# Attention scores as three 64-row products in two halves of TensorE's array, pairs taken two at a time, z turned by VectorE

## The chip, the cores and the metric

One core of a Trainium2 chip runs the whole kernel. The metric is the device time of one execution in microseconds (us), the median of three runs. Engines are called TensorE (PE in the rows; PEld is its weight loads), VectorE (DVE), ScalarE (ACT), GpSimd (POOL) and SyncE (SP, which issues the DMAs; SPq is its queue).

## What is computed

An attention without softmax over two batches of 3008 tokens, then two networks of two layers on its result. All arrays are float32 (the weights arrive as float64 and are converted by the kernel).

```
def _attn_ref(u, v, z):                      # u, v: (2, 3008, 256), z: (2, 3008, 64)
    scores = (1.0 / S) * np.matmul(z, z.transpose(0, 2, 1))
    attn = np.maximum(scores, 0.0) ** 2
    out = np.matmul(attn, v)
    return u * out
def _moe_ref(x, w_in, w_out):                # 256 -> 2048 -> 256
    h = x @ w_in
    return (h - np.tanh(h)) @ w_out
# second network: g = h from 1 up, 0 from -1 down, (h + 1)^2 / 4 between; g @ w_out
```

## The kernel before

Every float32 operand is split into hi (12 significant bits) and lo (the rest), and a product is the sum of float32r products of such parts: ScalarE copies hi, VectorE subtracts to get lo (`split`, line 87).

The attention is a list of 144 pairs (b, c, t): batch b, chunk c of 512 queries (the last chunk has 448), and two tiles of 128 keys. For each pair `attn_s` (line 283) makes the scores of two key tiles against the query chunk in one two-bank PSUM tile `sc`: z is held with its 64 hi rows over its 64 lo rows (`zs`) and the other way round (`zw`), so that two 128-row products (lines 293, 294) take all four terms; four products a pair. ScalarE then makes r = relu(sc / S) (line 300) and hi = r squared (302), VectorE a = r times r (301) and lo = a - hi (303). Two pairs later (LAG) `attn_av` (line 307) makes 12 products with v (line 316) into `acc`. After 12 pairs of a chunk VectorE multiplies acc by the turned u (342).

The order of the work is the order of the program on each engine. The loop of line 557 does for each pair i: `pump(i)` (line 516), which starts and advances loads; the hooks (loads of u, line 247, and its turning, 266); `attn_s` of pair i; `attn_av` of pair i - 2; and some steps of the weights' conversion on VectorE. `flush` at the end of `attn_s` issues the lo halves of splits of loads, which `split` had put off.

Loads of z, v and later the weights go through four buffers of the pool `raw` (line 58), taken in turn, and end in one of 18 slots of `ring`. The DMA of a load is issued on SP's queue, in order, and waits there until the buffer's former content was split. z comes in groups of 1024 tokens: one DMA, a split, eight 128x128 transposes on TensorE (line 143) into a PSUM tile of the scores' pool, a copy to `zs`, and two DMAs that make `zw` (154, 155). Tokens are ordered with partition p holding tokens 23p to 23p + 22, so that a DMA reads long pieces; the 64 tokens left over of each batch are a tile of their own.

The two networks follow, 96 pairs each, with 24 products a pair on TensorE.

Of the kernel before, what the change touches and what calls it, by code (L numbers as in the profile page):

```python
# [8 lines left out]
F32 = mybir.dt.float32  # L9
F32R = mybir.dt.float32r  # L10
# [16 lines left out]
def attention_then_two_ffn(  # L27
# [21 lines left out]
    assert D == 2 * P and DQ == 64 and REST == 64 and NFULL % 2 == 1 and B == 2  # L49
    NT = B * S // P  # L50
# [9 lines left out]
    tmp_p = ctx.enter_context(tc.tile_pool(name="tmp", bufs=2))  # L60
    sp_p = ctx.enter_context(tc.tile_pool(name="split", bufs=3))
# [3 lines left out]
    ident0 = const.tile([P, P], F32, name="ident0")  # L65
    ident = const.tile([P, P], F32R, name="ident")
# [9 lines left out]
    loads = []  # L76
    deferred = []   # VectorE's halves of splits: a pair later than ScalarE's
# [23 lines left out]
    def load_z(b, g):  # L101
        """Group g of 8 token tiles of z: [zh; zl] and [zl; zh], columns are tokens."""
        st = {}

        def dma(at=0, n=8):
            t = st["raw"] = raw_p.tile([P, 512], F32, tag="raw", name=f"zraw{b}_{g}_{at}")
            t3 = t.rearrange("p (t d) -> p t d", d=DQ)
            whole = min(n, NFULL - 8 * g - at)
            t0 = 8 * g + at
            nc.sync.dma_start(  # L110
                out=t3[:, :whole, :],
                in_=z[b, : NFULL * P, :].rearrange("(p t) d -> p t d", t=NFULL)[:, t0 : t0 + whole, :],
            )
            if whole < n:
                for h in range(2):
                    nc.sync.dma_start(out=t3[64 * h : 64 * h + 64, whole, :], in_=z[b, NFULL * P :, :])
            return t3

        def cut(at=0, n=8):
            t3 = st["raw"].rearrange("p (t d) -> p t d", d=DQ)  # L120
            zn = st["zn"] = sp_p.tile([P, 1024], F32R, tag="hi", name=f"zn{b}_{g}_{at}")
            if n < 8:
                zn = zn[:, : 3 * n * DQ].rearrange("p (t h d) -> p t h d", h=3, d=DQ)
            else:
                zn = zn.rearrange("p (t h d) -> p t h d", h=2, d=DQ)
            st["zn"] = zn
            split(zn[:, :, 0, :], zn[:, :, 1, :], t3[:, :n], now=(n < 8))
            if n < 8:
                nc.scalar.activation(out=zn[:, :, 2, :], in_=t3[:, :n], func=AF.Copy)

        def turn(at=0, n=8):
            flush()
            zn = st["zn"]
            ps = ps_s.tile([P, 2, 512], F32, tag="s", name=f"zps{b}_{g}_{at}")
            pw = ps_a.tile([P, 2, 512], F32, tag="acc", name=f"zpw{b}_{g}_{at}") if n < 8 else ps
            if at == 0:
                a = ring.tile([P, 1024], F32R, tag="w", name=f"zs{b}_{g}")
                w = ring.tile([P, 1024], F32R, tag="w", name=f"zw{b}_{g}")
                zs[b, g] = (a, w)
            a, w = zs[b, g]  # L140
            for i in range(8):
                h, k = divmod(i, n)
                nc.tensor.transpose(  # L143
                    (pw if h else ps)[:, i // 4, (i % 4) * P : (i % 4 + 1) * P].bitcast(F32R),
                    zn[:, k, h : h + 2, :].rearrange("p h d -> p (h d)"),
                    ident,
                )
            c = slice(at * P, (at + n) * P)
            got = ps.rearrange("p a n -> p (a n)")[:, : n * P]
            nc.scalar.activation(out=a[:, c], in_=got, func=AF.Copy)  # L150
            if n < 8:
                nc.vector.tensor_copy(out=w[:, c], in_=pw[:, 1, :])
            else:
                nc.sync.dma_start(out=w[0:64, c].bitcast(F32), in_=a[64:128, c].bitcast(F32))
                nc.sync.dma_start(out=w[64:128, c].bitcast(F32), in_=a[0:64, c].bitcast(F32))

        return [(dma, AHEAD), (cut, 3 if b + g == 1 else 4), (turn, 1 if b + g == 1 else 2)]

    def load_v(b, t):
        """Token tiles 2t and 2t+1 of v: hi and lo. The rest's tile holds hi over lo instead."""  # L160
        st = {}

        def dma():
            r = st["raw"] = raw_p.tile([P, 512], F32, tag="raw", name=f"vraw{b}_{t}")
            r3 = r.rearrange("p (t d) -> p t d", d=D)
            n = min(2, NFULL - 2 * t)
            nc.sync.dma_start(
                out=r3[:, :n, :],
                in_=v[b, : NFULL * P, :].rearrange("(p t) d -> p t d", t=NFULL)[:, 2 * t : 2 * t + n, :],
            )  # L170
# [71 lines left out]
    NPA = (NFULL + 1) // 2  # L242
    QC = (S + 511) // 512
# [3 lines left out]
    def load_u(b, c, j):  # L247
        """u transposed in blocks of 32: the load places the blocks, VectorE turns each."""
        n = min(4, NFULL - 4 * c)
        if j == 0:  # L250
            us[b, c] = (u_p.tile([P, 4, 4, 2, 32], F32, tag="ub", name=f"ub{b}_{c}"), n)
# [362 lines left out]
```

## Time and profile before

| what | value |
|---|---|
| median of 3 runs | 1570.79 us (1570.47 to 1572.19) |
| span of the profiled execution | 1569.2 us |
| PE busy | 1559.3 us (99%) |
| DVE busy | 1103.8 us (70%) |
| ACT busy | 777.4 us (50%) |
| chain that ended last | PE 99% |

The profiled execution's own time is not listed beside its span; the runs' median lies 1.6 us above the span, which is what lies around it. The scores' lines 293 and 294 are 8% of the chain that ended last, the products with v (316) 24%, the networks' products 67%. The attention ends, and the first network's products begin, at 519 us.

### The profile page before, as it was taken

The numbers are of one execution on the slowest core, as the hardware profiler recorded it, in microseconds if no ns is written. First come the engines' busy times: TensorE is split into PE (matmuls) and PEld (weight loads), VectorE is DVE, ScalarE is ACT, GpSimd is POOL, SyncE is SP. The second block draws the span as 40 slices with busy tenths as digits, with TensorE's granted clock in tenths as the row PEclk, the third lists the DMA queues.
The fourth block names the chain that finished last, engine by engine and source line by source line (L and its number), as shares of the span: only waits on it lengthen the run. The fifth ranks groups of instructions, "written<-read, shape, count | busy, mean of one in ns | idle before, by whom it ended". The sixth has DMA issues, their size and how long they took to land.

```text
span 1569.2 us, 19350 instructions
## 1 busy us (share of the span) xinstructions
PE 1559.3 (99%) x8057; PEld 1349.3 (86%) x8057; DVE 1103.8 (70%) x1132; ACT 777.4 (50%) x797; POOL 1.2 (0%) x7
## 2 busy tenths in 40 slices
PE   8999999999999999999999999999999999999998
PEld 6888889888888888888888888999999999999998
DVE  7888888888888966665665444477666666666665
ACT  7655557655556644444444444454444444444443
POOL 0000000000000000000000000000000000000000
PEclk9999999999999999999999999999999999999999
DMA  5121124221222311100101000020000000000000
GB/s 134 51 51 40 35 57 118 66 57 31 54 54 67 113 41 41 41 29 33 41 28 34 0 1 7 14 61 14 14 1 14 14 14 14 14 14 14 1 15 24
DMA packets 77400, 57.62 MB, mean 37 GB/s; under 512 B 54272, under 2 KB 55552, under 8 KB 77312
## 3 DMA queue, kind: packets, MB, share of 16 engines
q1 hardware_dynamic: 77312, 56.38, 12.6%
q8 instruction: 63, 1.03, 0.3%
q14 instruction: 25, 0.20, 0.0%
HBM read 39.19 MB, written 14.55 MB: 34 GB/s over the span
## 4 chain that ended last, share of the span: by engine, by line
PE 99%; DVE 0%; DMA 0%; ACT 0%; issue 0%; POOL 0%; SPq 0%; DVEq 0%; POOLq 0%
PE acc L316 24%; PE acc L416 17%; PE acc L396 16%; PE h L364 11%; PE h L365 11%; PE h L366 11%; PE sc L293 4%; PE sc L294 4%; PE zps L143 0%; PE warm L499 0%; DMA zw<-zs 0%; DVE lo L303 0%; DVE a L301 0%; ACT r L300 0%; PE zpw L143 0%
## 5 line engine op out<-in xcount | busy, mean ns | idle before, releaser
L88 ACT ACTIVATE gh<-g 128x1024 fp32r<-128x1024 f32 (+1 forms) x192 | 200.3, 1043 | 269.4 <-DVE g L383 141.3
L364 PE MATMUL h<-xl,w_in 128*128 128x512 f32 (+1 forms) x768 | 296.4, 386 | 0.0
L365 PE MATMUL h<-xh,w_in 128*128 128x512 f32 (+1 forms) x768 | 296.4, 386 | 0.0
L366 PE MATMUL h<-xh,w_in 128*128 128x512 f32 (+1 forms) x768 | 295.4, 385 | 0.0
L316 PE MATMUL acc<-hi,v 128*128 128x512 f32 (+1 forms) x1128 | 274.9, 385 | 0.0
L91 DVE TENSOR_TENSOR gl<-g,gh 128x1024 fp32r<-128x1024 f32 (+1 forms) x192 | 230.0, 1198 | 61.6 <-ACT gh L88 61.6
L316 PEld LDWEIGHTS acc<-hi,v 128*128 128x128 f32 x1128 | 211.7, 188 | 39.9 <-ACT hi L302 0.3
L378 DVE TENSOR_SCALAR t<-h 128x1024 f32<-128x1024 f32 (+1 forms) x96 | 115.4, 1202 | 170.9 <-PE h L366 170.9
L300 ACT ACTIVATE r<-sc 128x1024 f32<-128x1024 f32 (+1 forms) x144 | 145.4, 1010 | 175.0 <-PE sc L294 174.8
L375 DVE TENSOR_TENSOR g<-h,t 128x1024 f32<-128x1024 f32 (+1 forms) x96 | 115.4, 1202 | 146.2 <-ACT t L373 146.2
L301 DVE TENSOR_TENSOR a<-r 128x1024 f32<-128x1024 f32 (+1 forms) x144 | 172.5, 1198 | 49.8 <-ACT r L300 49.6
L416 PEld LDWEIGHTS acc<-w_out,gh 128*128 128x128 f32 x1504 | 192.8, 191 | 6.7
L416 PE MATMUL acc<-w_out,gh 128*128 128x256 f32 x1504 | 195.4, 283 | 0.0
L303 DVE TENSOR_TENSOR lo<-a,hi 128x1024 fp32r<-128x1024 f32 (+1 forms) x144 | 173.3, 1203 | 19.8 <-ACT hi L302 1.1
L396 PE MATMUL acc<-gh,w_out 128*128 128x512 f32 (+1 forms) x768 | 186.4, 385 | 0.0
L381 ACT ACTIVATE t<-t 128x1024 f32<-128x1024 f32 (+1 forms) x96 | 100.1, 1043 | 162.4 <-DVE t L378 162.4
L373 ACT ACTIVATE t<-h 128x1024 f32<-128x1024 f32 (+1 forms) x96 | 96.8, 1008 | 159.9 <-PE h L366 159.7
L366 PEld LDWEIGHTS h<-xh,w_in 128*128 128x128 f32 x768 | 144.3, 188 | 28.2
L396 PEld LDWEIGHTS acc<-gh,w_out 128*128 128x128 f32 x768 | 143.4, 188 | 27.5
L364 PEld LDWEIGHTS h<-xl,w_in 128*128 128x128 f32 x768 | 144.6, 188 | 25.3
L365 PEld LDWEIGHTS h<-xh,w_in 128*128 128x128 f32 x768 | 144.5, 188 | 24.2
L302 ACT ACTIVATE hi<-r 128x1024 fp32r<-128x1024 f32 (+1 forms) x144 | 150.4, 1045 | 9.2 <-PE acc L316 2.6
(61 smaller groups left out, 1421.1 us busy)
## 6 DMA issues: line engine op xcount, KB each, us to landing
wide_in<-in_moe_w_in_dram SPq DMA_DIRECT2D x16, 512.0 KB, 3.8
wide_out<-in_moe_w_out_dram SPq DMA_DIRECT2D x16, 512.0 KB, 3.8
vraw<-in_v_dram SPq DMA_DIRECT2D x22, 256.0 KB, 2.9
ub<-in_u_dram SPq DMA_DIRECT2D x160, 32.0 KB, 2.2
out_dram<-o SPq DMA_DIRECT2D x10, 512.0 KB, 2.6
w_in<-m_in SPq DMA_DIRECT2D x16, 256.0 KB, 2.2
w_out<-m_out SPq DMA_DIRECT2D x16, 256.0 KB, 2.1
wraw_in<-w_in SPq DMA_DIRECT2D x16, 256.0 KB, 2.9
```

What stands on the lines that cost most here:

```text
L88: nc.scalar.activation(out=hi, in_=src, func=AF.Copy)
L91: nc.vector.tensor_tensor(out=lo, in0=src, in1=hi.bitcast(F32), op=ALU.subtract)
L300: nc.scalar.activation(out=r[s], in_=ps[s], func=AF.Relu, scale=SCALE)
L301: nc.vector.tensor_tensor(out=a[s], in0=r[s], in1=r[s], op=ALU.mult)
L302: nc.scalar.activation(out=hi[s], in_=r[s], func=AF.Square)
L303: nc.vector.tensor_tensor(out=lo[s], in0=a[s], in1=hi.bitcast(F32)[s], op=ALU.subtract)
L316: nc.tensor.matmul(acc[:, d, :n], lhsT, g[:, j, :n], start=start, stop=stop)
L364: nc.tensor.matmul(ps[:, j, :n], w[:, 0, k, fs], xl[:, k, :n], start=(k == 0), stop=False)
L365: nc.tensor.matmul(ps[:, j, :n], w[:, 1, k, fs], xh[:, k, :n], start=False, stop=False)
L366: nc.tensor.matmul(ps[:, j, :n], w[:, 0, k, fs], xh[:, k, :n], start=False, stop=(k == 1))
L396: nc.tensor.matmul(acc[:, d, :n], w[:, part, j, d * P : (d + 1) * P], g[:, j, :n], start=start, stop=stop)
L416: nc.tensor.matmul(acc4[:, tt, :], g[:, j, tt * P : (tt + 1) * P], w[:, part, j, :], start=start, stop=stop, skip_group_check=True,)
```

## The change

z is loaded in groups of 512 tokens, in natural order, as 32x32 blocks by four DMAs: the two halves of its 64 columns, each to two places, so that the partitions 64 to 127 hold the same as 0 to 63. VectorE turns each block (`zt`), and hi and lo of it are two halves of one slot of the ring. The transposes on TensorE, the identity and the two DMAs for `zw` are gone. A group of z is loaded by one step (`work`) that issues its turning and both halves of its split at once.

The scores of a pair are six products of 64 rows: hi by hi, hi by lo, lo by hi, each for key tile 0 on partitions 0 to 63 and key tile 1 on partitions 64 to 127. `attn_s` takes two pairs: 12 products, two relus, two squares in place, two splits (hi is now a copy of a, after the square), and then two `attn_av`. The pools are: `tmp` one tag in 3 buffers (before two tags in 2), `split` 4 buffers (before 3), `raw` 4 as before. u, v and the output are in natural order: two DMAs of u for each step (before four or six), one store for each chunk. The networks write g in place of t. The start loads z, v 0 and v 1, with 7 products of zeros meanwhile.

```
-WARM = (6, 3)
+GROUP = 2
+WARM = 7
+QT = 512
...
+    zt_p = ctx.enter_context(tc.tile_pool(name="zt", bufs=1))
+    tmp_p = ctx.enter_context(tc.tile_pool(name="tmp", bufs=3))
+    sp_p = ctx.enter_context(tc.tile_pool(name="split", bufs=LAG + GROUP))
...
     def load_z(b, g):
...
+        def dma():
+            r = st["raw"] = raw_p.tile([P, QT], F32, tag="raw", name=f"zraw{b}_{g}")
+            r3 = r.rearrange("p (c e) -> p c e", e=32)
+            n = min(QT, S - QT * g) // 32
+            for i in range(4):
+                d = slice(32 * (i % 2), 32 * (i % 2) + 32)
+                at = slice(32 * i, 32 * i + 32)
+                nc.sync.dma_start(
+                    out=r3[at, :n, :],
+                    in_=z[b, QT * g : QT * g + 32 * n, d].rearrange("(c a) e -> a c e", a=32),
                 )
+                if 32 * n < QT:
+                    nc.sync.dma_start(
+                        out=r3[at, n:, :], in_=z[b, S - REST :, d].rearrange("(c a) e -> a c e", a=32)
+                    )
+
+        def work():
+            zt = zt_p.tile([P, QT], F32, tag="zt", name=f"zt{b}_{g}")
+            nc.vector.transpose(out=zt, in_=st["raw"])
+            w = ring.tile([P, 2, QT], F32R, tag="w", name=f"z{b}_{g}")
+            split(w[:, 0, :], w[:, 1, :], zt, now=True)
+            zs[b, g] = w
+
+        return [(dma, AHEAD), (work, 2)]
...
-            nc.tensor.matmul(ps[:, j, :n], zw[:, k0 : k0 + P], q, start=True, stop=False)
-            nc.tensor.matmul(ps[:, j, :n], za[:, k0 : k0 + P], q, start=False, stop=True)
...
+    def attn_s(todo):
+
+        got = []
+        for b, c, t in todo:
+            n = min(QT, S - QT * c)
+            ps = ps_s.tile([P, 2, 512], F32, tag="s", name="sc")
+            q = zs[b, c]
+            for k, (x, y) in enumerate(((0, 0), (0, 1), (1, 0))):
+                for j in range(2):
+                    half = slice(64 * j, 64 * j + 64)
+                    g, k0 = divmod((2 * t + j) * P, QT)
+                    nc.tensor.matmul(
+                        ps[:, j, :n], zs[b, g][half, x, k0 : k0 + P], q[half, y, :n], start=(k == 0), stop=(k == 2)
+                    )
+            got.append((ps, n))
+        out = []
+        for ps, n in got:
+            s = (slice(None), slice(None), slice(0, n))
+            a = tmp_p.tile([P, 2, 512], F32, tag="t1", name="a")
+            nc.scalar.activation(out=a[s], in_=ps[s], func=AF.Relu, scale=SCALE)
+            out.append((a, s, n))
+        for a, s, _ in out:
+            nc.vector.tensor_tensor(out=a[s], in0=a[s], in1=a[s], op=ALU.mult)
+        held = []
+        for a, s, n in out:
+            hi = sp_p.tile([P, 2, 512], F32R, tag="hi", name="hi")
+            lo = sp_p.tile([P, 2, 512], F32R, tag="lo", name="lo")
+            split(hi[s], lo[s], a[s], now=True)
+            held.append((hi, lo, n))
         flush()
...
+        for group in order:
+            for i in group:
+                pump(i)
+                for fn, args in hooks.get(i, ()):
+                    fn(*args)
+            i = group[0]
+            if i < NATT:
+                held.update(zip(group, attn_s([pairs[i][2] for i in group])))
...
+            for i in group:
+                if i >= LAG:
+                    _, av_fn, args = pairs[i - LAG]
+                    av_fn(*args, *held.pop(i - LAG))
+                make(i)
```

How TensorE's program reads, first in the kernel before, in the first chunk of batch 0 (`sc` are scores, `acc` the products with v, `zps` the transposes of z).

```order
L316 MATMUL acc<-hi,v_3_251 128x512 x8
L316 MATMUL acc<-lo,v_3_251 128x512 x4
L143 MATMUL zps_2_0_357<-ident,zn_2_0_287 128x128 x8
L293 MATMUL sc<-zs_0_125,zw_1_239 128x512
L294 MATMUL sc<-zs_0_125,zs_1_238 128x512
L293 MATMUL sc<-zs_0_125,zw_1_239 128x512
L294 MATMUL sc<-zs_0_125,zs_1_238 128x512
L316 MATMUL acc<-hi,v_4_285 128x512 x8
```

And in the changed kernel, at the same place.

```order
L251 MATMUL sc<-z_0_125,z_3_260 128x512 x12
L281 MATMUL acc<-hi,v_4_256 128x512 x8
L281 MATMUL acc<-lo,v_4_256 128x512 x4
L281 MATMUL acc<-hi,v_5_273 128x512 x8
L281 MATMUL acc<-lo,v_5_273 128x512 x4
L251 MATMUL sc<-z_0_125,z_4_337 128x512 x12
```

Twelve 64-row products stand between 24 products of 128 rows; no transpose is left on TensorE.

VectorE's program in the first chunk of the kernel before (line 91 is the lo half of a split of z, `zn`, or of v).

```order
L301 TENSOR_TENSOR a<-r 128x1024
L303 TENSOR_TENSOR lo<-a,hi 128x1024
L91 TENSOR_TENSOR v_4_285<-vraw_4_175,v_4_285 128x512
L91 TENSOR_TENSOR zn_2_0_287<-zraw_2_0_279,zn_2_0_287 128x8x64
L301 TENSOR_TENSOR a<-r 128x1024
L303 TENSOR_TENSOR lo<-a,hi 128x1024
L91 TENSOR_TENSOR v_5_323<-vraw_5_235,v_5_323 128x512
```

VectorE's program in the first chunk of the changed kernel (line 123 turns z, line 90 is the lo half of a split).

```order
L262 TENSOR_TENSOR a<-a 128x1024 x2
L90 TENSOR_TENSOR lo<-a,hi 128x1024 x2
L90 TENSOR_TENSOR v_4_256<-vraw_4_153,v_4_256 128x512
L90 TENSOR_TENSOR v_5_273<-vraw_5_190,v_5_273 128x512
L123 STREAM_TRANSPOSE zt_4_335<-zraw_4_268 128x512
L90 TENSOR_TENSOR z_4_337<-zt_4_335,z_4_337 128x512
L262 TENSOR_TENSOR a<-a 128x1024 x2
L90 TENSOR_TENSOR lo<-a,hi 128x1024 x2
```

The turning of a z block now stands between the lo halves of v of one group of pairs and the squares of the next one.

SP's queue around these loads in the kernel before (line 110 loads z, 167 v, 259 u; 154 and 155 make `zw`).

```order
L167 DMA vraw_5_235<-in_v_dram 128x512
L154 DMA zw_1_239<-zs_1_238 64x1024
L155 DMA zw_1_239<-zs_1_238 64x1024
L110 DMA zraw_2_0_279<-in_z_dram 128x448
L116 DMA zraw_2_0_279<-in_z_dram 64x64 x2
L167 DMA vraw_6_283<-in_v_dram 128x512
L259 DMA ub_0_289<-in_u_dram 32x8x32 x4
```

And in the changed kernel (112 loads z, 138 v, 226 u).

```order
L138 DMA vraw_5_190<-in_v_dram 128x2x256
L112 DMA zraw_3_192<-in_z_dram 32x16x32 x4
L138 DMA vraw_6_254<-in_v_dram 128x2x256
L226 DMA ub_0_263<-in_u_dram 32x16x32 x2
L138 DMA vraw_7_266<-in_v_dram 128x2x256
L112 DMA zraw_4_268<-in_z_dram 32x16x32 x4
```

A load of z, four DMAs now, follows every second load of v. Between vraw_5 and zraw_4 the pool `raw` of four buffers serves zraw_3, vraw_6 and vraw_7, so zraw_4 takes the buffer that vraw_5 had.

## Rows read from the trace of the kernel before

**Rows 1.** The page, part 1: busy us (share), instructions of each engine.

```profile
PE 1559.3 (99%) x8057; PEld 1349.3 (86%) x8057; DVE 1103.8 (70%) x1132; ACT 777.4 (50%) x797; POOL 1.2 (0%) x7
```

**Rows 2.** Windows, attention after batch 0's first chunk: busy us, clock, DMA share, GB/s.

```profile
50.80:269.00 218.20, 218.20 (x993) 184.28 (x992) 187.74 (x204) 131.43 (x134) 0.00 (x0) 1.00 0.21 54
```

**Rows 3.** Timeline of PE, one steady pair: start, duration, operation.

```profile
300.52 0.39 PE L293 MATMUL sc<-zs,zw 128*128 128x512 f32 x1
...
301.42 1.98 PE L316 MATMUL acc<-hi,v 128*128 128x512 f32 x8
...
304.14 0.39 PE L293 MATMUL sc<-zs,zw 128*128 128x512 f32 x1
```

**Rows 4.** Timeline of PE, 448 queries, and transposes of z.

```profile
257.20 0.37 PE L293 MATMUL sc<-zs,zw 128*128 128x448 f32 x1
...
258.02 1.81 PE L316 MATMUL acc<-hi,v 128*128 128x448 f32 x8
...
260.50 0.79 PE L143 MATMUL zps<-ident,zn 128*128 128x128 f32 x8
261.13 0.43 PE L293 MATMUL sc<-zs,zw 128*128 128x448 f32 x1
```

**Rows 5.** Groups by form: busy, mean ns, then idle before.

```profile
L293 PEld LDWEIGHTS sc<-zs,zw 128*128 128x128 f32 x288 | 54.1, 188 | 12.8 <-issue 2.3 <-ACT r L300 0.6
```

**Rows 6.** Timeline of PE, the first products after a wait.

```profile
21.71 0.47 PE L293 MATMUL sc<-zs,zw 128*128 128x512 f32 x1 [1.88 <-DMA zw<-zs]
22.02 0.39 PE L294 MATMUL sc<-zs,zs 128*128 128x512 f32 x1
```

**Rows 7.** Groups by form on DVE and ACT in the attention.

```profile
L303 DVE TENSOR_TENSOR lo<-a,hi 128x1024 fp32r<-128x1024 f32 x120 | 147.1, 1225 | 16.3 <-DVE a L301 0.5 <-ACT hi L302 0.4
L301 DVE TENSOR_TENSOR a<-r 128x1024 f32<-128x1024 f32 x120 | 146.4, 1220 | 42.9 <-ACT r L300 42.6
L302 ACT ACTIVATE hi<-r 128x1024 fp32r<-128x1024 f32 x120 | 127.5, 1063 | 6.7 <-ACT r L300 1.3 <-PE acc L316 0.8 <-DVE zn L91 0.8
L300 ACT ACTIVATE r<-sc 128x1024 f32<-128x1024 f32 x120 | 123.4, 1028 | 154.4 <-PE sc L294 154.4
L91 DVE TENSOR_TENSOR v<-vraw,v 128x512 fp32r<-128x512 f32 x22 | 15.0, 684 | 0.2 <-ACT v L88 0.2
L88 ACT ACTIVATE v<-vraw 128x512 fp32r<-128x512 f32 x22 | 13.5, 617 | 0.8 <-DMA vraw<-in_v_dram 0.8
L270 DVE STREAM_TRANSPOSE ut<-ub 128x512 f32<-128x512 f32 x20 | 13.0, 687 | 0.0
```

**Rows 8.** Timeline of DVE, back to back.

```profile
300.42 1.23 DVE L303 TENSOR_TENSOR lo<-a,hi 128x1024 fp32r<-128x1024 f32 x1
301.56 1.30 DVE L270 STREAM_TRANSPOSE ut<-ub 128x512 f32<-128x512 f32 x2
```

**Rows 9.** Timeline of ACT and DVE, a relu and its square.

```profile
308.88 1.03 ACT L300 ACTIVATE r<-sc 128x1024 f32<-128x1024 f32 x1 [1.50 <-PE sc L294]
...
309.94 1.23 DVE L301 TENSOR_TENSOR a<-r 128x1024 f32<-128x1024 f32 x1 [0.37 <-ACT r L300]
```

**Rows 10.** Line 259, u in blocks of 128-byte pieces: issue ns min/median/max; landing.

```profile
L259 SPq DMA_DIRECT2D ub<-in_u_dram x192: 312/449/1807, 22.3 to 508.2; - x192
...
DMA to landing us min/median/max: 1.7/2.2/4.4
```

**Rows 11.** Waits of SP's queue: for whom, us in total, times, longest.

```profile
SPq L167 <- DVE zn L91: 12.5, 4, 6.0
```

**Rows 12.** Timeline of PE, products with v of pairs 2 and 10.

```profile
22.70 1.98 PE L316 MATMUL acc<-hi,v 128*128 128x512 f32 x8
...
52.47 0.84 PE L316 MATMUL acc<-hi,v 128*128 128x512 f32 x3
```

**Rows 13.** Timeline of SP, the last stores.

```profile
1565.33 0.33 SPq L427 DMA_DIRECT2D out_dram<-o  x1
1565.71 1.19 SPq L434 DMA_DIRECT2D out_dram<-o  x2
```

More of the change, by code (lines that the diff above doesn't have):

```diff
@@ L6 @@
 from concourse._compat import with_exitstack
-from concourse.masks import make_identity
 F32 = mybir.dt.float32
@@ L103, in load_z @@
         st = {}
[L105 to L146, printed above, removed]
-                )
[L148 to L155, printed above, removed]
@@ L328, in attn_av @@
         ut, _ = us.pop((b, c))
-        g0 = NFULL * b + 4 * c
-        pieces = []
-        full = min(n, (NFULL - 4 * c) * P)
         o = 0
-        while o < full:
-            g, r = divmod(g0 * P + o, 512)
-            k = min(full - o, 512 - r)
-            pieces.append((g, r, o, k))
-            o += k
-        if full < n:
-            g, r = divmod(B * NFULL * P + b * REST, 512)
-            pieces.append((g, r, full, n - full))
-        for g, r, o, k in pieces:
+        while o < n:
+            g, r = divmod(b * S + QT * c + o, 4 * P)
+            k = min(n - o, 4 * P - r)
             nc.vector.tensor_tensor(
@@ L449, in ffn_av @@
         nc.scalar.activation(out=o[:, :nt, :], in_=acc4[:, :nt, :], func=AF.Copy)
-        store(o, 0, nt)
+        nc.sync.dma_start(
+            out=out[4 * P * c : 4 * P * c + n, :].rearrange("(t p) d -> p t d", p=P), in_=o[:, :nt, :]
+        )
     pairs = []
@@ L464, in attention_then_two_ffn @@
         for t in range(NPA):
-            if t == 0 or t % 4 == 2 and t + 2 < NPA:
-                g = (t + 2) // 4
-                last = end if 4 * g + 4 >= NPA else lastc + 4 * g + 3
-                add_load(base + 4 * g, last, load_z(b, g), slots=2)
+            if t % 2 == 0:
+                g = t // 2
+                add_load(base + t, end if g == QC - 1 else lastc + t + 1, load_z(b, g))
             add_load(base + t + LAG, lastc + t + LAG, load_v(b, t))
@@ L532, in pump, with make @@
                     n += 1
-        zl, v0, v1 = loads.pop(0), loads.pop(0), loads.pop(0)
-        zdma, zcut, zturn = (fn for fn, _ in zl["steps"])
-        warm(WARM[0])
-        zdma(0, 4)
-        zcut(0, 4)
-        zturn(0, 4)
-        zdma(4, 4)
-        v0["steps"][0][0]()
-        v1["steps"][0][0]()
-        zcut(4, 4)
-        v0["steps"][1][0]()
-        flush()
-        warm(WARM[1])
-        zturn(4, 4)
-        v1["steps"][1][0]()
-        flush()
-        live.extend([zl["last"]] * 2 + [v0["last"], v1["last"]])
-        held = {}
-        credit = 0.0
-        begin, step = NPA, 0
-        change = (NPA * QC - 6, NPA * QC + 10)
-        for i in range(len(pairs) + LAG):
-            pump(i)
-            for fn, args in hooks.get(i, ()):
-                fn(*args)
-            if i < len(pairs):
+        first = [loads.pop(0) for _ in range(3)]
+        for ld in first:
+            ld["steps"][0][0]()
+        warm(WARM)
+        for ld in first:
+            ld["steps"][1][0]()
+            live.append(ld["last"])
+        flush()
+        held = {}
+        state = {"credit": 0.0, "step": 0}
+        def make(i):
+            if begin <= i < change[0] or i >= change[1]:
+                state["credit"] += CONVERT[0] if i < NPA * QC * B else CONVERT[1]
+            while converts and state["credit"] >= 1:
+                state["credit"] -= 1
+                state["step"] += 1
+                if state["step"] == 1:
+                    next(converts[0])
+                elif state["step"] == 5 and len(converts) > 1:
+                    next(converts[1])
+                if next(converts[0], "end") == "end":
+                    converts.pop(0)
+                    state["step"] = 1
+        begin = NPA
+        change = (NPA * QC - 6, NPA * QC + 10)
+        NATT = B * QC * NPA
+        order = [range(i, i + GROUP) for i in range(0, NATT, GROUP)]
+        order += [range(i, i + 1) for i in range(NATT, len(pairs) + LAG)]
+        for group in order:
[6 more added lines that the diff above has]
+                held.update(zip(group, attn_s([pairs[i][2] for i in group])))
+            elif i < len(pairs):
                 s_fn, _, args = pairs[i]
```

102 lines of the change are left out of this document (16 added, 86 removed).

## The prediction

> **What bounds the kernel now.** Read first the busy shares: PE works for 99% of the span, DVE for 70%, ACT for 50% [rows 1]. Then the windows: in the attention PE has no idle time at all in 218 us, and DVE is busy for 187.74 of them, 86% [rows 2]. So the attention lasts as long as its products, and DVE is the next bound behind it, close. The timeline of one steady pair gives the period: 300.52 to 304.14, 3.62 us for 16 products of 512 columns, 0.227 each [rows 3]; with 448 columns the four score products take 0.82 us, 0.205 each [rows 4]. The networks are left as they are on PE, so the sum is made over the attention.
>
> **Score products.** Before, a pair takes 4 x 0.227 = 0.907 us of them. If the two 64-row products run side by side, the six take three places: 0.680. From the product with v of pair 2 on, which starts at 22.70 [rows 12], the scores of 139 pairs are still to come before (24 of them with 448 queries): 115 x 0.907 + 24 x 0.82 = 124.0 us. After, with two pairs a turn, it is 138: 114 x 0.680 + 24 x 0.615 = 92.3. That removes 31.7 us. Nothing before uses half of the array, so whether the halves run side by side stands in no row; the bounds are three places and six, and I take three, since the six products alternate between the halves and write different banks.
> By the Trainium skill, page TensorE: Matmul & The Clock Gate, section Part 3: Packing small matmuls, products on different row groups run concurrently; no run here shows it yet. By this rule the 31.7 stands, without it the third rival below.
>
> **Transposes of z.** Four groups of eight come after 22.70, each 0.63 us on PE (260.50 to 261.13) [rows 4]: 2.5 us gone.
>
> **Switching the array.** After 22.70 there are 69 turns, each with one switch to halves and one back. A product of 512 columns is shown for 0.389 us but the next starts after 0.227, so 0.16 us of it is still under way then [rows 3]. A product that starts after a wait delays the next to 0.31 (21.71 to 22.02) instead of 0.227, 0.085 more, because its weights were not loaded under another product [rows 6]. If each switch lets the array run empty and then loads weights in the open, it costs 0.16 + 0.085 = 0.25, a turn 0.5, and the sum 69 x 0.5 = 34.5 us. The ends: nothing (a gain is excluded, a switch removes no work), and 2 x (0.16 + 0.188) + 0.188 = 0.89 a turn with whole weight loads in the open, one more for the second half (0.188 each [rows 5]). I take 0.5, which the two rows on waits give, and not the ends.
> No row shows a switch of the array. By the Trainium skill, page TensorEngine Tiling (Array Packing), section Tiling Modes, a change of the tiling mode drains TensorE. By it the sum holds 0.33 to 0.89 a turn; without it only a lag of the second half, about 0.1, which is the first rival.
>
> **The loop through the buffers of `raw`.** This is the part that the diff does not show. The order of DVE in the first chunk is: squares and lo halves of two pairs, lo halves of two tiles of v, then the turning of a z block, its lo half, then the next squares. The block zraw_4 takes the buffer of vraw_5, so its four DMAs wait in SP's queue until the lo half of v 5 is done, and the turning of that block stands on DVE right behind this lo half and ahead of the next squares. So DVE, with all that is queued behind it (squares, lo halves), waits out the whole load; ACT's relus stand behind the hi half of the block and wait too, and with them the products with v. That SP waits on such buffers already before, up to 6.0 us at a time, is in its waits [rows 11].
> The round, from one lo half of v to the same one a turn later: three issues at 0.45 and a landing of 2.2 behind the fourth (from the loads of u in such blocks [rows 10]) 3.55; turning 0.69; hi half of z 0.62 and of the second v 0.62 on ACT; relu 1.03; two squares 1.14 + 1.22; hi 1.06; lo 1.22; two lo halves of v 1.3 [rows 7, 8]. That is 12.4. A hand-over from one queue to the next is 0.03 where a relu ends at 309.91 and its square starts at 309.94 [rows 9]; ten of them at up to twice that, an estimate, make the round 13.0. PE needs per turn 6 x 0.227 + 24 x 0.227 + 0.5 = 7.3. Three turns of batch 0 (z 3, 4 and 5) have this round: 3 x 5.7 = 17.1 us that PE waits. The turn after them has the loads of v 10 and v 11 behind the eight DMAs of z 5: eight issues at 0.45 are 3.6, I put 4 us. The bounds of the landing are 1.7 and 4.4 [rows 10], of an issue, which has twice the pieces, 0.31 and twice 0.45: the round is 12.1 to 16.5 and the three turns cost 14 to 28.
> At the change of batches the ring frees slots a turn earlier, the z block is there in time, and the round has no DMA in it. DVE itself is late then: turning 0.61, wait for hi of z 0.7, lo 0.61, wait for the relu behind the hi half of v 1.1 (0.62 + 1.03 - 0.61), squares 2 x 1.14, lo 2 x 1.14, v 1.2, together 8.8, and in two of four turns 1.22 more for turning u and for the product with u: 9.4 against 7.3. Four turns: 8.4 us.
> Elsewhere DVE has 2 x 2.37 = 4.7 us in a turn and some 1.9 for conversions and u, 6.6 of 7.3: hidden; with cheap switches (6.8) it just fits.
>
> **Start and end.** z's four DMAs, issued from 0.73, land at some 4.3; turning, hi, scores, and a second block that ACT and DVE must do before the first relu put the product with v of pair 2 at some 24.0, where before it starts at 22.70 [rows 12]: 1.3 us. At the end one store takes the place of three, whose last two are issued until 1566.90 [rows 13]: 1 us gone. Place of g in t, natural order and the larger pools cost nothing: the networks keep PE full with ACT at half load, and a buffer is written again three pairs later.
>
> **Sum.** -31.7 - 2.5 + 34.5 + 17.1 + 4 + 8.4 + 1.3 - 1 = +30.1. The span 1569.2 becomes 1599.3; the runs' median is 1.6 above the span, so 1601 us. With c us for the switches of a turn the sum is -0.9 + 62c, because in the seven late turns (three and four) PE waits anyway and a switch there costs nothing.
>
> **Rivals.**
> 1. Switches are almost free, 0.1 a turn: -0.9 + 6.2, 1576 us. For it: nothing in the trace has PE stop between unlike products, the transposes run into scores at 260.50 to 261.13 without a gap [rows 4]. Against: these use the same 128 rows.
> 2. The loop through `raw` does not bite, because loads land ahead of the turning: then -31.7 - 2.5 + 1.3 - 1 = -33.9, and the switches of all 69 turns against it. With 0.33 a turn 22.8, so 1560 us, faster; it is the better one as long as a turn's switches cost under 0.49. For it: before, loads of v kept pace with PE at 3.63 us a pair. Against: the order on DVE and SP, in which buffer and turning stand in one ring, whatever the DMA takes.
> 3. The halves run one after the other: 57 turns x 1.36 + 12 x 1.23 = 92 us more, of which some 9 fall in late turns: 30.1 + 83, 1684 us. Against: nothing but the alternating order.
> 4. The load of a z block costs more than that of u (twice the issue, landing 4.4) or the switch its upper end: 0.89 gives -0.9 + 55, 1625 us; 11 us more from the loads gives 1612; both 1636.
>
> **How the numbers follow.** Chances: the sum, with 0.33 to 0.65 a turn and 1590 to 1610 us, 0.50; rival 1 0.16; rival 2 0.10; rival 3 0.10; rival 4 0.14. The time is that of the first, 1601. The range 1571 to 1640 leaves out rival 3 and most of rival 2, some 0.2. What a measurement tells from no change is about 0.2%, 3.1 us: faster by more comes from rival 2 with a switch of up to 0.4 a turn and a little of rival 1, 0.10; within it 0.06 (rival 2 with 0.45 to 0.53, rival 1 with less than 0.06); slower 0.84.
>
> **What would show it.** In the timeline of PE: 12 score products of a turn starting in pairs a few ns apart, in 1.36 us; between the last of them and the first product with v, and back, starts 0.4 to 0.5 apart instead of 0.227. In the first chunk, PE idle some 6 us a turn in three turns, DVE's turning (line 123) waiting for the DMA of zraw, and the product with v of pair 10 at some 75 us instead of 52.47 [rows 12]. In batch 1's first chunk PE idle some 2 us in four turns, ended by ACT. Wrong would be: score products at 0.227 in sequence; turns of 6.8 us throughout; line 123 never waiting for a DMA; or idle stretches of PE after which 512-column products start further apart than 0.227, a lower clock, which the sum leaves out, since the granted clock reads 1.00 before [rows 2].

## The result and the profile after

The changed kernel takes 1593.59 us, the median of four runs (1591.45 to 1594.5), against 1570.87 for the kernel before beside it: 1.0139 times as long, 95% interval 1.0125 to 1.0154. Forecast were 1601 us in a range of 1571 to 1640. The profiled execution took 1594.5 us with a span of 1592.7, 23.5 more than the span before.

First part 1 of the page: busy time (share of the span) and instructions of each engine, where [rows 1] stood before.

```profile
PE 1565.3 (98%) x8287; PEld 1312.6 (82%) x8287; DVE 1106.2 (69%) x1140; ACT 766.4 (48%) x793; POOL 0.7 (0%) x5
```

PE is busy 6.0 us longer, though the score products of a pair were to take three places instead of four (busy time also counts products that a lower clock made longer, see below), and the other 17.5 us of the 23.5 are time in which it waits. A timeline of PE shows where the loss ends: this is the first product of the networks, before and after (start, duration, operation, idle time before it and what ended it).

```profile
519.13 0.39 PE L364 MATMUL h<-xl,w_in 128*128 128x512 f32 x1
```

```profile
543.05 0.50 PE L321 MATMUL h<-xl,w_in 128*128 128x512 f32 x1 [1.38 <-ACT a L259]
```

From 519.13 to 543.05, 23.9 us are lost up to here, and the stretch behind it is 0.4 us shorter. Everything has to be looked for in the attention.

A steady turn (two pairs, without a wait), in PE's timeline. Line 251 is the scores, line 281 the products with v; it answers to [rows 3].

```profile
178.01 1.66 PE L251 MATMUL sc<-z 64*128 64x512 f32 x12
179.60 2.11 PE L281 MATMUL acc<-hi,v 128*128 128x512 f32 x8
181.55 1.07 PE L281 MATMUL acc<-lo,v 128*128 128x512 f32 x4
182.46 1.98 PE L281 MATMUL acc<-hi,v 128*128 128x512 f32 x8
184.27 1.07 PE L281 MATMUL acc<-lo,v 128*128 128x512 f32 x4
185.27 1.66 PE L251 MATMUL sc<-z,z 64*128 64x512 f32 x12
```

From start to start a turn is 185.27 - 178.01 = 7.26 us. Read it by starts, not by durations, since a product's end is still under way when the next begins. The twelve products with 64 rows occupy 1.59 us, little more than six places of 0.227 (1.36), so the two halves of the array work side by side. The first block of eight hi products takes 181.55 - 179.60 = 1.95, the second 184.27 - 182.46 = 1.81; the lo block ahead of the scores takes 1.00, the other 0.91. So 30 places of 0.227 make 6.81, and the switches add 0.45 a turn: 0.09 ahead of the score block, 0.23 from its first product to the first one with v, 0.13 in the block behind that. Two pairs before took 2 x 3.62 = 7.24 us [rows 3]: a turn gains nothing.

Narrow windows of the same timeline show single products at the two borders of the block that starts at 185.27: the last lo product, the second pair of scores, the last pair, and the second product with v.

```profile
184.95 0.39 PE L281 MATMUL acc<-lo,v 128*128 128x512 f32 x1
185.60 0.40 PE L251 MATMUL sc<-z,z 64*128 64x512 f32 x2
186.53 0.39 PE L251 MATMUL sc<-z,z 64*128 64x512 f32 x2
187.19 0.40 PE L281 MATMUL acc<-hi,v 128*128 128x512 f32 x1
```

At either border the first product starts 0.32 after the one before it (184.95 to 185.27, 186.53 to 186.85), and the second 0.33 to 0.34 after the first (to 185.60, to 187.19). These four steps are some 0.40 us over 4 x 0.227; the rest of the 0.45 is in the steps right behind them.

The weight loads (PEld) of the same place show what goes with it.

```profile
184.04 0.87 PEld L281 LDWEIGHTS acc<-lo,v 128*128 128x128 f32 x4
185.26 1.23 PEld L251 LDWEIGHTS sc<-z,z 64*128 64x128 f32 x12 [0.35 <-issue]
186.85 1.68 PEld L281 LDWEIGHTS acc<-hi,v 128*128 128x128 f32 x8 [0.36 <-issue]
```

At both switches the loads pause for 0.35 us, and the first load starts in the same instant as its block (185.26 and 185.27; 186.85 and 186.85). Where nothing is switched, the loads of lo run 0.23 ahead of their products (184.04 and 184.27).

Batch 0's first chunk, PE again: the products with v around the three late turns, for [rows 12].

```profile
22.51 0.49 PE L281 MATMUL acc<-hi,v 128*128 128x512 f32 x1
24.06 1.89 PE L281 MATMUL acc<-hi,v 128*128 128x512 f32 x7 [1.05 <-DVE v L90]
...
37.75 3.35 PE L281 MATMUL acc<-hi,v 128*128 128x512 f32 x7 [2.20 <-DVE v L90]
40.90 1.91 PE L281 MATMUL acc<-lo,v 128*128 128x512 f32 x4
...
49.99 2.78 PE L281 MATMUL acc<-hi,v 128*128 128x512 f32 x7 [1.84 <-DVE v L90]
...
63.57 2.73 PE L281 MATMUL acc<-hi,v 128*128 128x512 f32 x7 [2.50 <-DVE v L90]
66.10 1.85 PE L281 MATMUL acc<-lo,v 128*128 128x512 f32 x4
67.79 2.00 PE L281 MATMUL acc<-hi,v 128*128 128x512 f32 x8
...
72.21 2.10 PE L281 MATMUL acc<-hi,v 128*128 128x512 f32 x8
```

From the first product with v of pair 2 to that of pair 10 it is 49.70 us, where the kernel before took 29.77 [rows 12]. Of pairs 2, 4, 6 and 8 the first product runs alone, and the second waits for DVE's lo half of v; these second ones start at 24.06, 37.75, 49.99 and 63.57, so the late turns are 13.69, 12.24 and 13.58 us long. What DVE does meanwhile:

```profile
23.32 1.29 DVE L90 TENSOR_TENSOR v<-vraw,v 128x512 fp32r<-128x512 f32 x2
29.55 0.71 DVE L123 STREAM_TRANSPOSE zt<-zraw 128x512 f32<-128x512 f32 x1 [4.95 <-DMA zraw<-in_z_dram]
...
32.39 2.36 DVE L262 TENSOR_TENSOR a<-a 128x1024 f32<-128x1024 f32 x2 [0.74 <-ACT a L259]
...
37.01 1.29 DVE L90 TENSOR_TENSOR v<-vraw,v 128x512 fp32r<-128x512 f32 x2
41.79 0.71 DVE L123 STREAM_TRANSPOSE zt<-zraw 128x512 f32<-128x512 f32 x1 [3.49 <-DMA zraw<-in_z_dram]
```

It stands idle 4.95 and 3.49 us for a block of z, with the squares of the turn behind it. And the other half of the ring: the issue of that second load of z on SP's queue (zraw_4), and the waits of the queue from 22 to 75 us (waiter, released by, us in total, times, longest):

```profile
37.77 1.90 SPq L112 DMA_DIRECT2D zraw<-in_z_dram  x4
```

```profile
SPq L112 <- DVE v L90: 21.1, 3, 7.0
```

The loads of z wait for DVE's lo half of v, and DVE waits for the loads of z. One detail differs from the section on the change, which gave zraw_4 the buffer of vraw_5: zraw_4 goes out at 37.77, while DVE is still busy with the second of the two lo halves, that of v 5, until 38.30 (37.01 + 1.29). So it had waited for the lo half of v 4 alone. The ring is closed all the same, 0.6 us earlier. In the windows view the granted clock of this stretch is 0.83 (busy times of PE, PEld, DVE, ACT, POOL; then clock, DMA share, GB/s):

```profile
22.50:72.20 49.70, 37.65 (x146) 26.34 (x144) 31.23 (x36) 22.59 (x30) 0.00 (x0) 0.83 0.39 85
```

Behind idle time the seven hi products from 37.75 stand 0.45 apart, which is the lower of the two levels (1.2 GHz), instead of 0.227.

At the change of batches, PE:

```profile
281.87 1.66 PE L251 MATMUL sc<-z 64*128 64x512 f32 x12
...
290.07 1.88 PE L251 MATMUL sc<-z,z 64*128 64x512 f32 x12 [1.90 <-ACT a L259]
...
299.74 1.88 PE L251 MATMUL sc<-z,z 64*128 64x512 f32 x12 [1.58 <-ACT a L259]
```

Four turns of 8.20, 9.67, 8.07 and 8.02 us, ended by ACT, whose relus wait behind z.

### The profile page after: what moved, and what is told of

It reads as the page before. It is cut to its first block, busy times and chain, and to the rows that moved or that the text cites. A ratio compares the mean times of both kernels' runs of the same rounds, so it can differ in the third digit from the quotient of the medians.

```text
span 1592.7 us, 19671 instructions
## 1 busy us (share of the span) xinstructions
PE 1565.3 (98%) x8287; PEld 1312.6 (82%) x8287; DVE 1106.2 (69%) x1140; ACT 766.4 (48%) x793; POOL 0.7 (0%) x5
## 4 chain that ended last, share of the span: by engine, by line
PE 92%; DVE 3%; ACT 2%; DMA 1%; issue 1%; SPq 1%; DVEq 0%; ACTq 0%
PE acc L281 21%; PE acc L372 17%; PE acc L352 16%; PE h L321 11%; PE h L322 11%; PE h L323 11%; PE sc L251 6%; DVE a L262 2%; ACT a L259 1%; DVE lo L90 1%; ACT hi L87 1%; DMA vraw<-in_v_dram 1%; DMA zraw<-in_z_dram 1%; SPq L112 0%; DVE v L90 0%
## 5 line engine op out<-in xcount | busy, mean ns | idle before, releaser
L87 ACT ACTIVATE gh<-t 128x1024 fp32r<-128x1024 f32 (+1 forms) x192 | 200.3, 1043 | 268.4 <-DVE t L339 140.2
L281 PE MATMUL acc<-hi,v 128*128 128x512 f32 (+1 forms) x1128 | 289.9, 399 | 9.5 <-DVE v L90 7.6
L90 DVE TENSOR_TENSOR gl<-t,gh 128x1024 fp32r<-128x1024 f32 (+1 forms) x192 | 229.9, 1198 | 61.6 <-ACT gh L87 61.6
L331 DVE TENSOR_TENSOR t<-h,t 128x1024 f32<-128x1024 f32 (+1 forms) x96 | 115.3, 1202 | 146.2 <-ACT t L329 146.2
L262 DVE TENSOR_TENSOR a<-a 128x1024 f32<-128x1024 f32 (+1 forms) x144 | 166.6, 1198 | 67.8 <-ACT a L259 67.4
L259 ACT ACTIVATE a<-sc 128x1024 f32<-128x1024 f32 (+1 forms) x144 | 137.1, 1004 | 140.4 <-PE sc L251 140.4
L87 ACT ACTIVATE hi<-a 128x1024 fp32r<-128x1024 f32 (+1 forms) x144 | 150.4, 1044 | 36.2 <-DVE a L262 31.3
L90 DVE TENSOR_TENSOR lo<-a,hi 128x1024 fp32r<-128x1024 f32 (+1 forms) x144 | 166.8, 1200 | 0.2
```

Of the source, the lines that this page charges most:

```text
L87: nc.scalar.activation(out=hi, in_=src, func=AF.Copy)
L90: nc.vector.tensor_tensor(out=lo, in0=src, in1=hi.bitcast(F32), op=ALU.subtract)
L259: nc.scalar.activation(out=a[s], in_=ps[s], func=AF.Relu, scale=SCALE)
L262: nc.vector.tensor_tensor(out=a[s], in0=a[s], in1=a[s], op=ALU.mult)
L281: nc.tensor.matmul(acc[:, d, :n], lhsT, g[:, j, :n], start=start, stop=stop)
L331: nc.vector.tensor_tensor(out=t1[s], in0=ps[s], in1=t1[s], op=ALU.subtract)
```

## The experiments

Two questions: is it the loop through the buffers that costs the first chunk (and not the turning on DVE as such), and what is the 0.45 us of a turn?

**Six buffers.** `raw` gets six buffers instead of four, and gives up one of the conversion's for the room.

```
-    cv_p = ctx.enter_context(tc.tile_pool(name="cv", bufs=2))
+    cv_p = ctx.enter_context(tc.tile_pool(name="cv", bufs=1))
-    raw_p = ctx.enter_context(tc.tile_pool(name="raw", bufs=4))
+    raw_p = ctx.enter_context(tc.tile_pool(name="raw", bufs=6))
```

> The changed kernel with six buffers for loads instead of four; the space comes from the conversion's two scratch tiles, one buffer each instead of two. Theory (the loop through the four buffers): a block of z is then loaded a whole turn before its turning, the three long turns of batch 0's first chunk (12.2 to 12.9 us) fall to about the steady 7.3, VectorE's wait of 17.8 us for zraw goes: 1593.6 - 17 to 21 = 1573 to 1577 us; batch 1's first chunk stays as it is. Rival (the place of the turning on VectorE, ahead of the squares, is the cause by itself, whatever the buffers): VectorE's wait only moves to the relus and the turns stay at 11 us or more: 1588 to 1594.

Measured: 1576.19 us, ratio to the kernel before 1.0032 (1.0020 to 1.0044), so 17.4 us under the changed kernel. SP's waits for loads of z from 22 to 75 us:

```profile
SPq L112 <- DVE v L90: 0.3, 2, 0.2
```

The same stretch in its windows view:

```profile
22.50:72.20 49.70, 46.04 (x218) 34.29 (x219) 43.67 (x50) 31.84 (x39) 0.00 (x0) 0.97 0.32 72
```

The wait of the z loads went from 21.1 us to 0.3, and DVE does not wait for a z in this stretch at all. The queue still waits 11.1 us for lo halves of v, but now with loads of v, which DVE does not need next. The granted clock came back to 0.97 with it: the low clock went with the waiting. From pair 2 to pair 10 PE now takes 35.4 us instead of 49.70. Four steady turns would be 29.0, so the loop is 14.3 of the 20.7 us that were lost there. In what is left PE waits 3.9 us for lo halves of v, and some of its products are slow. The other 3 us of the gain lie elsewhere (an earlier start, the change of batches, and no wait ahead of the networks), so the expected time was met in part by luck.

**Four buffers, squares first.** The turning and the split of z are kept in a list and issued behind the two squares of a turn (`mid`).

```
-        return [(dma, AHEAD), (work, 2)]
+        return [(dma, AHEAD), (later, 2)]      # later(): mid.append(work)
...
             nc.vector.tensor_tensor(out=a[s], in0=a[s], in1=a[s], op=ALU.mult)
+        for fn in mid or ():
+            fn()
+        mid = []
```

> The changed kernel with four buffers, but the turning and split of a z block stand behind the two squares of a turn instead of ahead of them. Theory (buffers): a z block's DMA still waits for the lo half of v of the turn before, so the round from one such lo half to the next keeps its length but for the two squares, which now lie beside the load: 12.2 to 12.9 us a turn become 10 to 12, the time 1584 to 1595. Rival (place on VectorE): the squares no longer wait, the long turns fall to 8 us or less: 1572 to 1578.

Measured: 1587.57 us, ratio 1.0106 (1.0089 to 1.0123), 6.0 us under the changed kernel. DVE:

```profile
24.38 2.35 DVE L270 TENSOR_TENSOR a<-a 128x1024 f32<-128x1024 f32 x2
29.12 0.71 DVE L124 STREAM_TRANSPOSE zt<-zraw 128x512 f32<-128x512 f32 x1 [2.38 <-DMA zraw<-in_z_dram]
```

The squares (line 270 here) fill part of the wait, 2.38 us of the 4.95 remain, and the loop stays closed. The order on DVE alone is not the cure.

**The control of the buffers.** The kernel before with the same two pool sizes.

```
-    cv_p = ctx.enter_context(tc.tile_pool(name="cv", bufs=2))
+    cv_p = ctx.enter_context(tc.tile_pool(name="cv", bufs=1))
-    raw_p = ctx.enter_context(tc.tile_pool(name="raw", bufs=4))
+    raw_p = ctx.enter_context(tc.tile_pool(name="raw", bufs=6))
```

> The control of the six buffers: the kernel before with six raw buffers and one buffer for the conversion. My theory (the loop through the raw buffers bites only in the changed kernel, where SyncE's loads of z wait for one): no change, 1568 to 1573 us. Rival (six buffers are worth some 17 us to any of these kernels, since loads start earlier): 1553 to 1560 us.

Measured: 1571.09 us, ratio 1.0001 (0.9992 to 1.0010). Six buffers are worth nothing where the loop does not exist.

**Scores without halves.** The tiles of z hold the same 64 dimensions in both halves, so products over all 128 rows give twice the sum.

```
-                    half = slice(64 * j, 64 * j + 64)
+                    half = slice(0, P)
...
-            nc.scalar.activation(out=a[s], in_=ps[s], func=AF.Relu, scale=SCALE)
+            nc.scalar.activation(out=a[s], in_=ps[s], func=AF.Relu, scale=SCALE / 2)
```

> The score products read all 128 rows instead of one half (z stands in both halves, so each sum comes out doubled, and relu's scale is halved): 12 products a turn, each alone in the array, and no switch between halves and whole array. My theory (a steady turn's 0.46 us over the plain count of products is paid for the halves: two switches and the two halves' skew): a turn is 36 x 0.227 = 8.17 us, 0.91 more than the 7.26 measured, over 69 to 72 turns 63 to 66 us more: 1650 to 1660 us. Rival (the 0.46 us come with any change from the products with v to the score products and back, halves or not): a turn of 8.63 us, 1685 to 1695 us.

Measured: 1644.9 us (one run). PE in a steady turn:

```profile
173.93 2.88 PE L251 MATMUL sc<-z,z 128*128 128x512 f32 x12
176.65 1.98 PE L281 MATMUL acc<-hi,v 128*128 128x512 f32 x8
...
182.09 2.88 PE L251 MATMUL sc<-z,z 128*128 128x512 f32 x12
```

Its weight loads (PEld) ahead of the second of these blocks:

```profile
181.87 2.68 PEld L251 LDWEIGHTS sc<-z,z 128*128 128x128 f32 x12
```

The turn is 8.16 us = 36 x 0.227, with nothing left over, and the loads start 0.22 ahead of their block. So the change from products with v to scores and back costs nothing by itself; the 0.45 us belong to the halves. The total came out under the 1650 to 1660 that I expected, mostly because I charged 0.91 to the late turns too. By the starts of the score blocks the five of the first chunk take 57.5 us here against 59.4 in the changed kernel, and the four at the change of batches 32.2 against 34.0: they had room for longer scores. Why they became shorter was not followed up; in the stretch from 22.5 to 72.2 us the granted clock was 0.93 here, against 0.83.

**Every score product twice.** 24 products with 64 rows in a block, with relu's scale halved.

```
-            for k, (x, y) in enumerate(((0, 0), (0, 1), (1, 0))):
+            for k, (x, y) in enumerate(((0, 0), (0, 0), (0, 1), (0, 1), (1, 0), (1, 0))):
```

> Each score product is issued twice into the same sum (relu's scale halved): 24 products with 64 rows in one block a turn instead of 12, the switches as before. My theory (most of the 0.46 us is paid once for a block, at its two ends): a turn is 7.26 + 6 x 0.227 = 8.62 us, 72 x 1.36 = 98 us more, less up to 8 in the first chunk's waits: 1683 to 1692 us. Rival (the block's 0.23 us over its plain count go with every product, 0.265 for two side by side): 7.26 + 1.59 = 8.85 us, 72 x 1.59 = 114 us more: 1699 to 1709 us.

Measured: 1675.62 us (one run). PE in a steady turn:

```profile
179.77 3.04 PE L251 MATMUL sc<-z,z 64*128 64x512 f32 x24
182.73 2.12 PE L281 MATMUL acc<-hi,v 128*128 128x512 f32 x8
...
188.42 3.04 PE L251 MATMUL sc<-z,z 64*128 64x512 f32 x24
```

The block takes 2.96 us instead of 1.59: twelve more products cost 1.37, or 0.114 each, half of 0.227. They run side by side, and the 0.23 us over the plain count is paid once a block. The turn is 8.65 against 8.62 and 8.85 expected. The total missed both ranges, again by the room in the late turns: the turns at the change of batches are 8.64 to 8.66 here, as long as any other, so PE does not wait there any more.

**An extra switch.** A product of zeros with 8 columns between the hi and the lo products of the first pair of a turn, once with 64 rows, once with 128 as control; it adds nothing to the sums.

```
+        if t % 2 == 0:
+            nc.tensor.matmul(acc[:, 1, :8], zero[:64, :P], zero[:64, :8], start=False, stop=False)
```

> The changed kernel with one more product in each turn: 64 rows of zeros, 8 columns, added to acc between the hi and the lo products of the first pair with v (it adds nothing to the result). It adds two switches of the array a turn. Theory (each border between 64 and 128 rows costs 0.23 us, by the steady turn of 7.26): against the same product with 128 rows (the other kernel of this pair) 0.46 more in each of 72 turns, 33 us, less some 3 in turns where PE waits anyway. Rival (the 0.23 belong to the 64-row products themselves, not to the switch): the same as the 128-row one within 3 us.

> The control of the kernel before it: the same added product of zeros with 128 rows, so without a switch. Both theories: 72 times a weight load and 8 columns, 0.03 to 0.15 us each, so 1596 to 1604 us; a steady turn of 7.3 to 7.4.

Measured: 1614.29 and 1603.61 us (one run each). PE with the product of 64 rows:

```profile
185.58 2.11 PE L281 MATMUL acc<-hi,v 128*128 128x512 f32 x8
187.62 0.18 PE L289 MATMUL acc<-zero 64*128 64x8 bf16 x1
187.73 1.20 PE L281 MATMUL acc<-lo,v 128*128 128x512 f32 x4
188.76 1.99 PE L281 MATMUL acc<-hi,v 128*128 128x512 f32 x8
```

And with the product of 128 rows:

```profile
190.01 2.11 PE L281 MATMUL acc<-hi,v 128*128 128x512 f32 x8
191.96 0.18 PE L289 MATMUL acc<-zero 128*128 128x8 bf16 x1
192.00 1.17 PE L281 MATMUL acc<-lo,v 128*128 128x512 f32 x4
193.00 1.99 PE L281 MATMUL acc<-hi,v 128*128 128x512 f32 x8
```

The control already costs 10.0 us, 0.14 a turn, and two switches add 10.7 us to it, 0.15 a turn. Neither my 33 us nor the rival's nothing came out. The control is no clean one, since the bf16 product among the others makes the lo products' first load open as well (193.00 - 192.00 = 1.00 instead of 0.91), and so takes part of the price before the switch comes. With 64 rows both neighbours of the added product are late: the hi block ahead of it lasts 2.04 (187.62 - 185.58) instead of 1.95, and the lo block behind it 1.03 instead of 0.91. With 128 rows the hi block keeps its 1.95 and only the lo block is late. So 0.15 a turn is what the switches add to a product that is already dear, not the whole price of two switches. Nor is a single product a block: of the four late steps of a turn (0.32 twice, 0.33 and 0.34) it has no second product of its own to be late. How much of 0.45 us is an array that runs empty and how much a load in the open stays unsettled; that it is paid once a block is what the run before shows.

**Both repairs.** Six buffers and the squares ahead of z, the two edits above together.

> Six raw buffers and z's turning and split behind the two squares at once. My theory: with six buffers the DMA is out of the loop, and what is left of the first chunk's loss are the three waits of TensorE for v's low part on VectorE (3.9 us) behind z's two gaps of 0.7 us a turn; with the squares ahead of z these gaps are filled, so 2 to 5 us less than six buffers alone: 1571 to 1574 us, within 0.2% of the kernel before. Rival (v's low part only comes later, since all of VectorE's work stays ahead of it): 1575 to 1578 us.

Measured: 1573.51 us, ratio 1.0015 (1.0006 to 1.0024), 2.7 us under six buffers alone. PE's waits for the low part of v (from 20 to 560 us) fell from 3.9 us to 2.6.

**The low part of v first.** The same, and `flush()`, which issues the low parts of v, moved from the end of the turn to ahead of the squares.

```
+        flush()
         for a, s, _ in out:
             nc.vector.tensor_tensor(out=a[s], in0=a[s], in1=a[s], op=ALU.mult)
...
-        flush()
```

> Two pairs a turn, six raw buffers, z's turning behind the squares, and v's low part ahead of the squares (the control of the three-pair kernel for the order on VectorE). My theory (the 2.6 us that TensorE still waits for v's low part in the first chunk go, since v's high part is long there while VectorE waits for relu): 1570 to 1573 us. Rival (VectorE is full in these turns, so the wait moves to the scores' low parts): 1573 to 1576 us.

Measured: 1572.67 us, ratio 1.0009 (1.0000 to 1.0018). The time lies in the theory's range, but only 0.8 us were gained: from 20 to 560 us PE's waits for v went, those for hi on ACT grew from 2.6 us to 4.0, and 1.5 us of waits for z came new. That part of the rival was right.

**Three pairs a turn.** If a block costs 0.45 whatever stands in it, fewer blocks are cheaper. PSUM has room for three score tiles if acc has one.

```
-LAG = 2
-GROUP = 2
+LAG = 3
+GROUP = 3
...
-            ps = ps_s.tile([P, 2, 512], F32, tag="s", name="sc")
+            ps = bank("s", ("p0", "p1", "p2"), "sc")     # acc: bank("a", ("p3",), "acc")
```

> Three pairs a turn instead of two: 48 score blocks of 18 products instead of 72 of 12, with three score tiles and a single acc tile in PSUM, six raw buffers, v's low part ahead of the squares and z's work behind the low parts. My theory (0.46 us are paid once a block): a turn of 3 pairs is 36 x 0.227 + 18 x 0.1135 + 0.46 = 10.7 us, and 24 blocks fewer are worth 11 us against the two-pair kernel with both repairs (1573.5): 1560 to 1566 us, 0.5% under the kernel before. Rival (the single acc tile makes each of the 11 borders between chunks wait for VectorE's emptying, 1.2 to 2.5 us each, beyond the 2.5 us of score products that lie there): 1571 to 1590 us.

Six buffers and the low part of v first are kept; z's work stands behind the low parts of the scores and may begin four pairs ahead instead of two, six loads may be under way instead of four, and four tiles each of hi and lo are left as they were.

Measured: 1576.1 us, ratio 1.0038 (1.0025 to 1.0052): by time the rival. A steady turn of PE, from start to start:

```profile
172.61 2.35 PE L264 MATMUL sc<-z,z 64*128 64x512 f32 x18
...
183.28 2.35 PE L264 MATMUL sc<-z,z 64*128 64x512 f32 x18
```

Its two longest waits of PE, at the start and at the change of batches:

```profile
17.64 4.21 PE L264 MATMUL sc<-z,z 64*128 64x512 f32 x18 [6.61 <-ACT a L272]
...
282.83 3.39 PE L297 MATMUL acc<-hi,v 128*128 128x512 f32 x8 [6.90 <-DVE x L314]
```

The turn is 10.67 us, 10.7 expected, so a block of 18 costs 10.67 - 36 x 0.227 - 9 x 0.227 = 0.46 as well. PE's busy time fell to 1549.0. But the time came back in waits. It is not the eleven borders of the rival: the emptying of acc makes PE wait at one, the change of batches, and the first relu stands behind z's tiles at the start.

**Three pairs, waits taken out.** z's work goes behind the squares inside a chunk and behind the emptying of acc at its border, and the fourth tile of z behind the first turn.

```
+        if todo[0][2] != 0:
+            run_mid()
         held = []
...
                 make(i)
+            run_mid()
```

> The three-pair kernel with its two large stalls taken on: z's work runs behind the squares and ahead of the low parts, but behind the emptying of acc at a border between chunks, and the fourth tile of z no longer stands ahead of the first relu. My theory (48 blocks save 11 us, and the three-pair kernel gave them back in waits: 6.6 us on the first relu, which stood behind a z on its way, 4 us for z in the first chunk, 6.9 us for the emptying behind two z's at the batch change): some 3 + 3 + 4 us of these go: 1563 to 1568 us, faster than the kernel before by 0.2 to 0.5%. Rival (VectorE has no room in these turns, and the waits only move to the low parts): 1571 to 1577 us.

Measured: 1568.07 us, ratio 0.9979 (0.9970 to 0.9988): faster than the kernel before by 0.2%, and just over the 1563 to 1568 that I expected. PE's waits on the emptying of acc and on the relu at the start fell from 6.9 and 6.6 us to 2.8 and 2.6; the largest that is left, up to 560 us, is 4.4 us for z.

## Why the prediction was right, and where its sizes were off

The forecast's mechanism held: the products gained pay for the switches, and the loop through `raw` and DVE's late turns are lost on top. One wait that it named did not come (the turn after the loop), and two terms came near by parts that offset each other.

- **Score products, 31.7 us gone.** Right: three places a pair, 0.114 a product with 64 rows. The third rival (halves in sequence) falls. The Trainium skill, page TensorE: Matmul & The Clock Gate, Part 3: Packing small matmuls, has products in different row groups run at the same time; by the twelve in 1.59 us the trace agrees.
- **Switching the array, 0.5 a turn.** 0.45, and so some 62 x 0.05 = 3.1 us less. At each border I had put 0.16 ahead of the first product (the array runs empty) and 0.085 behind it (a load in the open); by the starts it is 0.09 and 0.11. So the sum is closer than its parts, and the sign that I named, starts 0.4 to 0.5 apart at the border, did not come: they are 0.32 apart. The first rival falls (its 0.1 a turn came from no row). The Trainium skill, page TensorEngine Tiling (Array Packing), section Tiling Modes, says that a change of mode drains TensorE; that the cost goes where every product has 128 rows (8.16 = 36 x 0.227) agrees.
- **The loop through `raw`, three turns of 13.0 us.** 13.69, 12.24 and 13.58, so 0.5 us more in all, and with six buffers most of the loss went. That the size is so near is in part luck. From its first issue to its turning a load of z took 5.48, 4.02 and 5.35 us (the second from 37.77 to 41.79), where I had 3.55. Against that, it waits for one lo half of v and not for two (0.6 a turn), and the 0.6 a turn for hand-overs is not seen: from the turning to the next lo half of v it is 7.47 us (41.79 to 49.26), and my rows without any hand-over give 7.60.
- **The turn after, 4 us for loads of v.** PE waited for nothing there. It lost 1.7 us all the same, by the clock: the seven hi products from 63.57 stand 0.36 apart on average and the four lo products from 66.10 0.42, until 0.227 comes back at 67.79. That is 2.3 us less than I had.
- **Change of batches, 8.4 us.** 2.5 us too much. Over a turn without a wait the four lose some 1.9 (against 6.3, since its products with v are those with 448 queries), 2.4, 0.8 and 0.8: 5.9 us. I had put 1.22 more for u into two of the four turns; DVE's timeline has it in one, the second.
- **Start, 1.3 us later.** The first product with v of pair 2 came at 22.51, but the second only at 24.06. With 0.34 from a first to a second product that is a start at 23.72, 1.0 later than before.
- **Left out.** The networks' first product waits 1.38 us for the last relus of the attention, and the end gave 0.4 us back instead of 1.
- **Left out too, the clock.** It was granted at 0.83 in the first chunk, and the prediction named that as what could make it wrong. In the three late turns DVE's round sets the pace, and slow products lie within it; in the turn after they are the 1.7 us. No run took the clock away and left the loop.

By these: 30.1 - 3.1 + 0.5 - 2.3 - 2.5 - 0.3 + 1.4 + 0.6 = 24.4, against 23.5 between the spans; 0.9 stays unaccounted for. So the result is under the forecast by several small terms, most of them of one direction, and the two large ones, products and switches, were right.

The second rival deserves a last look. Its premise was false for the kernel as changed, but six buffers make it true. With 0.45 a turn its sum is -33.9 + 69 x 0.45 = -2.9, or 1568 us; the best two-pair version ran 1572.67. What is still between them is most likely DVE's and ACT's work on z and v in the first chunk of each batch, which that sum left out: PE's 5.5 us of waits from 20 to 560 us there are for hi and z on ACT.

## What to carry to other kernels

Count half-array products by blocks: here they ran at twice the rate, and each block of them cost 0.45 us, so that a block of twelve just paid for itself and one of eighteen was a gain. Before moving a transform from one engine to another, follow the ring of buffer, load and queue position: a load that waits for a buffer, freed by an instruction that stands shortly ahead of the load's own reader on the same engine, puts the whole transfer into every turn, and two buffers more took it out. Costs do not add up to the total in turns that already wait; the two experiments that made the scores longer came out 14 us (51 for 72 x 0.91 = 65) and 16 us (82 for 98) under the plain sum, mostly for that reason.

## What the runs showed of the hardware that was not expected

- The cost of a block with 64 rows hardly depended on its length: 0.45 us a turn with 12 products, 0.48 with 24 (8.65 - 8.17), 0.46 with 18. It lies in the first two products at either border: the first started 0.32 after the one before it, the second 0.33 to 0.34 after the first, instead of 0.227.
- One bf16 product with 8 columns among the others cost 0.14 us a turn, with 128 rows and no switch; with 64 rows 0.29.
- After idle time in the first chunk 512-column products stood 0.45 us apart, and the granted clock of that stretch was 0.83; with the waits gone it was 0.97.
